# Two token tiles of the first MLP block turned by VectorE instead of TensorE, and a reordering of the attention phase, in a two-layer linear-attention and MLP kernel

## The chip, the cores and the metric

The kernel runs on one core of a Trainium2 chip. The metric is device time of one execution in microseconds (us). Engines are named as in the profile: PE is TensorE, PEld its weight loads, DVE is VectorE, ACT is ScalarE, POOL is GpSimd, and SP is the engine that issues all of this kernel's DMAs, one after the other, from one queue. Each engine takes its instructions strictly in the order in which the program lists them.

## The reference, cut to what matters

The input x has 2048 tokens of 448 features, in float32. Two layers follow each other, each an attention step and an MLP step:

```python
x = x + attention(layernorm(x))       # phi(q) @ (phi(k)^T v), 16 heads of 28, divided by phi(q) . sum(phi(k)), then @ wo
x = x + mlp(layernorm(x))             # gelu(h @ w1 + b1) @ w2 + b2, hidden size 1792
phi = lambda t: where(t > 0, t + 1, exp(t)) + 1e-6
```

Both layers use the same weights. The output has the shape of x.

## The kernel before

**Precision.** A float32 product is made of three fast matmuls. Every operand is split into a high part (a rounded copy, written by ACT) and a low part (the rest, written by DVE or POOL); PE multiplies high by high, high by low and low by high. For the last 64 features two matmuls do.

**Tiles and phases.** The tokens are 16 tiles of 128, and 4 blocks of 4 tiles. A layer has three parts: `phase1` over the 16 tiles, a transition written out as the list of tokens `ORDER` (L491), and the MLP over 4 blocks (L933), in which the attention output of the next block is made beside the MLP of this one (`behind`, L861).

**phase1 (L542).** Step t runs the tokens of a string, `STEP` (L499), with own strings for step 0 and step 1. The tokens, each an operation on one tile:

- `a` takes the layer-norm statistics (DVE bn_stats, bn_aggr, an add; POOL a power, `brs`), `n` normalises (DVE, L383; ACT copies a tail of 64 features for tiles that PE transposes).
- `T` transposes a normalised tile on PE into a PSUM bank (L246); `X` splits it into `XH` (ACT) and `XL` (DVE). The first six tiles of layer 0 go this way. All other tiles are turned by DVE (`tu`, `tv`: L277, L278, 32x32 blocks), stored to DRAM (L283) and read back with the blocks in their places (`sp`, four DMAs, L289); then `X` is `split_t` (L291): ACT L295, DVE L296.
- `K` is the key projection of tile t (11 matmuls), `kp`, `kh`, `kl` its phi and its split (`kl` is DVE L440, followed by the running sum `za`, L444), `s` splits the tile the other way round (ACT L415, POOL L416 and L417), and `G` accumulates x^T phi(k) of tile t-1 in four PSUM banks with tag "acc" (11 matmuls, L479 to L483).
- `Q` is the query projection (11 matmuls) and `qp` its phi, stored to DRAM. Only the first `DEFER` tiles have their query here: 10, so that the six others stand as `Q` in `ORDER`.
- `bg` (layer 0 only) takes `BG[t]` pieces of the MLP weights: a DMA on SP in one step, ACT and POOL splitting it in the next.

Tile 2's transpose takes one of the four "acc" banks (L571), the one that the fourth accumulator of `G` needs next.

**Launch.** In layer 0 the first two tiles go through a hand-written order (`LAUNCH`, L508), and a few lines ahead of it (L896).

**ORDER.** `z`, `gt`, `kv`, `mask`, `m`, `ms` form the matrix M = (masked kv) wo and split it into `Mh` and `Ml`; `qz`, `qs`, `tq`, `qq` scale, transpose and split the queries of block 0; `o` multiplies them by M; `la` adds the residual and takes statistics, `lb` normalises (`o_n`, L744), `T` transposes (L754), `x` splits (L758). Between them stand the deferred `Q`, each followed later by `Qp` (phi on ACT and POOL, L462) or `Qv` (phi on ACT and DVE, L456). `pre` loads the queries of block 1. Then ACT loads the table for gelu (L929) and the MLP starts; its first matmuls need all four split tiles of block 0.

**Buffers that matter.** PSUM: tag "h" has 2 banks (queries, some transposes, MLP hidden), "m" 2, "acc" 4. SBUF: tag "S" has 5 buffers of 128x1024, for weight staging, M, and the turned tiles on their way to DRAM (`sq`) and back (`sp`).

Of the kernel before, what the change touches and what calls it, by code (L numbers as in the profile page):

```python
# [12 lines left out]
OP = mybir.AluOpType  # L13
# [9 lines left out]
def linear_attn_mlp_kernel(  # L23
# [38 lines left out]
    def bank(tag, bufs, name):  # L62
        return psum.tile([128, 512], F32, name=name, tag=tag, bufs=bufs)
# [127 lines left out]
    def ln_bn(xs):  # L191
        st = work.tile([128, 6], F32, name="bst", tag="bst", bufs=2)
        dve.bn_stats(st, xs)
        return st
# [39 lines left out]
    def block(key):  # L234
        if key not in blocks:
            blocks[key] = Block()
        return blocks[key]
# [10 lines left out]
    def split_x(key, j):  # L248
        tp = tps.pop((key, j))
        hi, lo = blocks[key].pieces(j)  # L250
        act.copy(hi, tp)
        dve.tensor_sub(lo, tp, f(hi))
# [35 lines left out]
        for m in range(4):  # L288
            sp.dma_start(r[m * 32:(m + 1) * 32].rearrange("r (i f) -> r i f", i=4), d[m])  # L289

    def split_t(key, t, hi, lo):  # L291

        x = spreads[key, t // 2].rearrange("p (i c u n) -> p u c i n", i=4, c=4, n=32)[:, t % 2]
        h = hi.rearrange("p (c i n) -> p c i n", c=4, n=32)
        act.copy(h, x)  # L295
        dve.tensor_sub(lo.rearrange("p (c i n) -> p c i n", c=4, n=32), x, f(h))  # L296


    def proj(name, key, j, o=None, cs=range(4)):
# [80 lines left out]
    def stage_n(l, t):  # L380

        xs, mv, rs = sts.pop((l, t))
        dve.tensor_scalar(xs, xs, mv[:, 0:1], rs, op0=OP.subtract, op1=OP.mult)  # L383
        xns[l, t] = xs
        if t < TURNED[l]:
            d = tails[l, t] = work.tile([128, 128], F32, name="tail", tag="tail", bufs=2)
            act.copy(d.rearrange("p (u n) -> p u n", u=2), xs[:, None, TL:].to_broadcast([128, 2, 64]))
# [60 lines left out]

    qs_ = {}

    def stage_q(l, t, cs=range(4)):
        qs_[l, t] = proj("q", ("a", l, t // 4), t % 4, qs_.get((l, t)), cs)
        if 3 in cs:
            qo.append((l, t, qs_.pop((l, t))))

    def stage_qphi():  # L456
        while qo:
            l, t, o = qo.pop(0)
            e = phi(o, "eq")
            sp.dma_start(pq_d[l][t * 128:(t + 1) * 128, :], e)  # L460

    def fill_qphi():  # L462

        l, t, o = qo.pop(0)
        e = t512("e", 3, "eq")[:, :D]
        p = t512("E", 2, "ep")[:, :D]
        act.activation(e, o, AF.Relu, scale=-1.0)
        act.activation(p, o, AF.Relu)
# [19 lines left out]

    ORDER = (  # L491
# [4 lines left out]
    )  # L496
    DEFER = NT - ORDER.split().count("Q")

    STEP = "qp K T X s a kp n kh tu kl tv G bg Q ld sp"  # L499
    STEP_0 = "K T X s kp kh kl a n tu Q ld sp"  # L500
    STEP_1 = "T a X qp s kh tu n kl tv G bg ld sp", STEP
    NORM = (
        ((2,), (3, 4), (5, 6), (7,), (8,), (9,), (10,), (11,), (12, 13), (14,), (15,)),
        ((5,), (6,), (7,), (8,), (9,), (10,), (11,), (12, 13), (14,), (15,)),
    )


    LAUNCH = (  # L508
        "kb0 ha0 hb0 ka1 kb1 n1 la0 lb0 K00 T1 K01 ha1 hb1 la1 lb1 ka2 kb2 K10 K11 ka3 kb3 qa0 qb0 K02 K12 K03 K13 "
        "qa1 qb1 qa2 qb2 Q00 Q10 Q01 Q11 Q02 Q12 s0 a2 kp0 qa3 qb3 kh0 n2 kl0 kp1 Q03 Q13"  # L510
    )
    PRE = 5
    BG = [0, 0, 1] + [2] * 5 + [1, 2] + [1] * 6
    LATE = sum(BG)
    loaded = {0: 3}

    def load_to(l, t):
# [24 lines left out]
    def phase1(l, tr):  # L542
        za = consts.tile([128, D], F32, name="za", tag="za")
        acc = []
        load_to(l, NORM[l][1][-1])
        if l == 0:
            launch(za)
            load_to(l, NORM[l][2][-1])
        for t in range(l == 0, NT):
            norm = NORM[l][t] if t < len(NORM[l]) else ()  # L550
            for tok in (STEP_0 if t == 0 else STEP_1[l] if t == 1 else STEP).split():
                if tok == "sp":
                    for u in norm:
                        if u % 2:
                            stage_sp(l, u)
                elif tok == "ld" and t + 2 < len(NORM[l]):
                    load_to(l, NORM[l][t + 2][-1])
                elif tok == "a":
                    for u in norm:
                        stage_a(l, u)  # L560
                elif tok == "n":
                    for u in norm:
                        stage_n(l, u)
                elif tok == "tu":
                    for u in norm[:1]:
                        stage_t(l, u)
                elif tok == "tv":
                    for u in norm[1:]:
                        stage_t(l, u)
                elif tok == "T" and t + 1 < NT:  # L570
                    stage_b(l, t + 1, "acc" if t == 1 else "h")  # L571
                elif tok == "X" and t + 1 < NT and (l == 0 or t + 1 >= 4):
                    stage_x(l, t + 1)
                elif tok == "K":
                    stage_k(l, t)
                elif tok == "qp":
                    stage_qphi()
                elif tok == "kp":
                    stage_kphi(l, t)
                elif tok == "kh":  # L580
                    stage_kh(l, t)
                elif tok == "kl":
                    stage_kl(l, t, za)
                elif tok == "s":
                    stage_s(l, t)
                elif tok == "G" and t >= 1:
                    acc = acc or [bank("acc", 4, f"G{c}")[:, :D] for c in range(4)]
                    stage_g(l, t - 1, acc)
# [56 lines left out]
    def trans_ms(tr, g):  # L645
        if g == 0:
            tr.Mh, tr.Ml = [], []
        if g % 2 == 0:
            for n in ("Mh", "Ml"):
                s = work.tile([128, 1024], F32R, name=n, tag="S", bufs=5)  # L650
                getattr(tr, n).extend(s[:G, i * D:(i + 1) * D] for i in range(2))
        act.copy(tr.Mh[g], tr.mp[g])
        dve.tensor_sub(tr.Ml[g], tr.mp[g], f(tr.Mh[g]))

# [89 lines left out]
    def o_n(l, b, j):  # L744
        t = b * 4 + j
        xn = xns["m", l, t] = ln_norm(sts.pop(("m", l, t)), f"xm{l}_{t}")
        if b == 0:
            act.copy(xn[:, D:], xn[:, TL:D])

    def add_bias(l, b, j):  # L750
# [153 lines left out]
    for l in range(LAYERS):  # L904
# [6 lines left out]
        def pre(j):  # L911
# [3 lines left out]
                background(2)  # L915

        tok_ = SimpleNamespace(
            Q=lambda j: stage_q(l, fill.pop(0)), Qp=lambda j: fill_qphi(), Qv=lambda j: stage_qphi(), G=lambda j: stage_g(l, NT - 1, acc),
            ld=lambda j: (load_pq(l, 0, j), load_x(l, j)), z=lambda j: trans_z(tr, za), gt=lambda j: trans_gt(tr, acc),
            kv=lambda j: trans_kv(tr), mask=lambda j: trans_mask(tr), m=lambda j: trans_m(tr, j),  # L920
            ms=lambda j: trans_ms(tr, j), qz=lambda j: q_z(l, 0, j, tr), qs=lambda j: q_scale(l, 0, j, tr),
            tq=lambda j: q_transpose(l, 0, j), qq=lambda j: q_split(l, 0, j), o=lambda j: o_mm(l, 0, j, tr),
            la=lambda j: o_ln(l, 0, j), lb=lambda j: o_n(l, 0, j), T=lambda j: m_transpose(l, 0, j),
            x=lambda j: m_split(l, 0, j), pre=pre)
# [71 lines left out]
```

## Time and profile before

| what | value |
|---|---|
| time of 3 runs | 881.01, 881.14, 884.27 us; median 881.14 |
| profiled execution | 881.78 us |
| its span (first to last instruction) | 880.1 us |
| granted TensorE clock | 1.000 |
| PE idle by the view of waits | 1.5 + 1.1 + 0.7 + 0.7 + 0.4 us |

The span by stretches (us of the trace, from the views of windows and timeline; busy time in us):

| stretch | what | us | PE | DVE | ACT | POOL | GB/s |
|---|---|---|---|---|---|---|---|
| 0 to 22.59 | launch and step 1, layer 0 | 22.59 | 18.74 | 15.17 | 13.94 | 11.72 | 152 |
| 22.59 to 70.73 | steps 2 to 8 | 48.14 | 48.14 | 38.21 | 31.13 | 25.38 | 189 |
| 70.73 to 104.49 | steps 9 to 15 | 33.76 | 33.72 | 24.50 | 23.70 | 22.27 | 215 |
| 104.49 to 141.18 | ORDER, layer 0 | 36.69 | 36.33 | 26.69 | 17.83 | 13.60 | 104 |
| 444.51 to 536.28 | phase1, layer 1 | 91.77 | 91.67 | 68.06 | 51.67 | 28.34 | 157 |
| 536.28 to 572.94 | ORDER, layer 1 | 36.66 | 36.30 | 26.67 | 16.89 | 11.35 | 80 |

A row of the timeline gives start, duration, engine, line, operation, tiles, shapes, count and, in brackets, the idle time of the engine before it and what the profile holds for its end. Matmuls overlap: one of 448 columns is listed with 0.37 us, but in a row of them each starts 0.20 us after the one before. So the pace of PE is read from the differences of starts, and a stall of less than about 0.17 us does not show as idle time.

### The profile page before, as it was taken

Reading aid. Unit: us, or ns where it says so; the run is one execution under the profiler, and the core shown is the slowest. Engines: PE = TensorE matmul, PEld = TensorE weight load, DVE = VectorE, ACT = ScalarE, POOL = GpSimd, SP = SyncE. Lnnn points to the kernel's source line nnn. Section 1 sums busy time; section 2 is a strip of 40 time slices with the busy share of each in tenths; the row PEclk is TensorE's granted clock in tenths of the full one; section 3 lists DMA queues with packets and bytes.
Section 4 is the critical chain, followed back from the end, with each engine's and each line's share of the span. In section 5 each row is a group of like instructions: output and inputs, shape, how many; then the busy total and the mean of one; then the engine's idle time right before and its main releaser. Section 6 shows DMA issues by size and latency. Waiting matters only on the chain.

```text
span 880.1 us, 11693 instructions
## 1 busy us (share of the span) xinstructions
PE 871.8 (99%) x4190; PEld 773.4 (88%) x4190; DVE 485.6 (55%) x947; ACT 344.8 (39%) x609; POOL 221.1 (25%) x252
## 2 busy tenths in 40 slices
PE   8999999999999999999999999999999999999998
PEld 6999988888888888888899999888888888888887
DVE  6878585658455543226467866755574473432112
ACT  6576645324223322333355664442233133223221
POOL 5466633335012102011222333220220140140000
PEclk9999999999999999999999999999999999999999
DMA  5477715624413402051146443243332323111001
GB/s 156 148 213 223 218 53 159 199 78 140 132 59 104 156 0 96 1 178 48 48 136 196 153 144 95 63 152 101 104 114 91 112 75 131 49 49 40 3 1 42
DMA packets 62762, 93.71 MB, mean 106 GB/s; under 512 B 8816, under 2 KB 57968, under 8 KB 62704
## 3 DMA queue, kind: packets, MB, share of 16 engines
q1 hardware_dynamic: 62704, 92.97, 33.7%
q8 instruction: 33, 0.54, 0.3%
q14 instruction: 25, 0.20, 0.1%
HBM read 55.65 MB, written 34.08 MB: 102 GB/s over the span
## 4 chain that ended last, share of the span: by engine, by line
PE 96%; DVE 1%; POOL 1%; DMA 1%; ACT 1%; issue 0%; SPq 0%; POOLq 0%; ACTq 0%; DVEq 0%
PE y L806 10%; PE y L805 10%; PE y L804 10%; PE hp L787 9%; PE hp L786 9%; PE hp L788 9%; PE hp L789 3%; PE hp L790 3%; PE G L480 2%; PE G L481 2%; PE G L479 2%; PE psk L306 2%; PE psk L308 2%; PE psk L307 2%; PE psq L306 2%; PE psq L307 2%
## 5 line engine op out<-in xcount | busy, mean ns | idle before, releaser
L796 DVE TENSOR_TENSOR gl<-g,gh 128x512 fp32r<-128x512 f32 x112 | 82.7, 738 | 299.7 <-ACT gh L795 299.7
L792 ACT ACTIVATE g<-hp,b1s 128x512 f32<-128x512 f32 x112 | 77.0, 688 | 406.4 <-PE hp L790 406.4
L806 PE MATMUL y<-w2h,gl 128*128 128x448 f32 x448 | 163.9, 366 | 0.0
L805 PE MATMUL y<-w2l,gh 128*128 128x448 f32 x448 | 163.8, 366 | 0.0
L804 PE MATMUL y<-w2h,gh 128*128 128x448 f32 x448 | 163.8, 366 | 0.0
L787 PE MATMUL hp<-XH,w1l 128*128 128x512 f32 x336 | 131.7, 392 | 0.0
L786 PE MATMUL hp<-XH,w1h 128*128 128x512 f32 x336 | 131.4, 391 | 0.0
L788 PE MATMUL hp<-XL,w1h 128*128 128x512 f32 x336 | 131.2, 391 | 0.0
L203 POOL TENSOR_TENSOR brs<-bve,mhalf 128x1 f32<-128x1 f32 x64 | 38.9, 607 | 272.5 <-DVE bve L201 265.4
L804 PEld LDWEIGHTS y<-w2h,gh 128*128 128x128 f32 x448 | 84.2, 188 | 8.8
L805 PEld LDWEIGHTS y<-w2l,gh 128*128 128x128 f32 x448 | 84.3, 188 | 8.3
L806 PEld LDWEIGHTS y<-w2h,gl 128*128 128x128 f32 x448 | 84.3, 188 | 6.5
L788 PEld LDWEIGHTS hp<-XL,w1h 128*128 128x128 f32 x336 | 63.1, 188 | 13.6
L787 PEld LDWEIGHTS hp<-XH,w1l 128*128 128x128 f32 x336 | 63.2, 188 | 11.1
L786 PEld LDWEIGHTS hp<-XH,w1h 128*128 128x128 f32 x336 | 63.3, 188 | 10.9
L795 ACT CAST gh<-g 128x512 fp32r<-128x512 f32 x112 | 69.7, 622 | 3.6
L416 POOL TENSOR_TENSOR xnl<-x,xnh 128x384 fp32r<-128x384 f32 x32 | 35.7, 1117 | 84.4 <-ACT xnh L415 50.0
L683 POOL TENSOR_TENSOR pz<-pq,zb 128x448 f32<-128x448 f32 x32 | 36.6, 1148 | 79.7 <-DVE dn L689 65.3
L296 DVE TENSOR_TENSOR XL<-sp,XH 128x512 fp32r<-128x512 f32 x50 | 42.7, 861 | 5.3 <-ACT XH L295 5.3
L790 PE MATMUL hp<-XL,w1x 128*128 128x512 f32 x112 | 43.6, 389 | 0.0
L789 PE MATMUL hp<-XH,w1x 128*128 128x512 f32 x112 | 43.6, 389 | 0.0
L752 POOL TENSOR_TENSOR x<-x,b2b 128x448 f32<-128x448 f32 x32 | 41.9, 1332 | 0.0
(145 smaller groups left out, 1565.6 us busy)
## 6 DMA issues: line engine op xcount, KB each, us to landing
x<-in_A_x_dram SPq DMA_DIRECT2D x32, 224.0 KB, 3.7
pq_d<-eq SPq DMA_DIRECT2D x32, 224.0 KB, 2.9
pq<-pq_d SPq DMA_DIRECT2D x32, 224.0 KB, 3.2
x<-x_d SPq DMA_DIRECT2D x32, 224.0 KB, 3.6
sq_a<-sq SPq DMA_DIRECT2D x13, 512.0 KB, 2.9
sp<-sq_a SPq DMA_DIRECT2D x52, 128.0 KB, 3.0
sq_q<-sq SPq DMA_DIRECT2D x12, 512.0 KB, 2.6
sp<-sq_q SPq DMA_DIRECT2D x48, 128.0 KB, 3.1
```

Of the source, the lines that this page charges most:

```text
L296: dve.tensor_sub(lo.rearrange("p (c i n) -> p c i n", c=4, n=32), x, f(h))
L786: pe.matmul(o, w1h[:, c, s], x.moving(x.hi, c), start=(c == 0), stop=False)
L787: pe.matmul(o, w1l[:, c, s], x.moving(x.hi, c), start=False, stop=False)
L788: pe.matmul(o, w1h[:, c, s], x.moving(x.lo, c), start=False, stop=False)
L789: pe.matmul(o, w1x[:, s], x.moving(x.hi, 3), start=False, stop=False)
L790: pe.matmul(o, w1x[:, s], x.moving(x.lo, 3), start=False, stop=True)
L792: act.activation(g, hp, AF.Gelu_apprx_tanh, bias=b1s[:, i:i + 1])
L795: act.copy(gh, g)
L796: dve.tensor_sub(gl, g, f(gh))
L804: pe.matmul(acc[j], gh[:, s], w2h[:, i], start=first, stop=False)
L805: pe.matmul(acc[j], gh[:, s], w2l[:, i], start=False, stop=False)
L806: pe.matmul(acc[j], gl[:, s], w2h[:, i], start=False, stop=last)
```

## The change

- **Launch.** Ahead of it, tile 0 is normalised (and its tail copied by ACT) before ACT splits the first key weight. In `LAUNCH`, `la0` (the low part of tile 0's first half) stands ahead of `n1`.
- **Step 1 of layer 0.** `X` of tile 2 stands ahead of the statistics; only tile 3 is taken in this step, tile 4 moves to step 2; the phi of the two first queries (`q1`) is spread out, the second one ahead of the normalisation of tile 3. Step 2 of layer 0 has its own string, with three tiles' statistics and the key's phi between them.
- **All other steps** from 2 in layer 0 and from 1 in layer 1: `kl` stands ahead of `tu`.
- **Queries.** Seven are deferred, so step 9 has no `Q`. In `ORDER` one `Q` stands between `o2` and `o3`, one after `o3`, and the last two (`Qa`) write to "acc" banks. The third `Qp` stands ahead of `ms0`; four queries now have their phi by `Qv`.
- **Block 0's tiles 0 and 1** in both layers: `tu0`, `tu1`, one store, one read back (`st`, `sp`), and `split_t` in place of PE's transposes `T0`, `T1` and of `split_x`; for tile 0 the subtraction is made by POOL. ACT copies no tail for them. `pre` moves behind `x2`.
- **Buffers.** The last two rows of `Ml` go to "F" buffers, and `sq`, `sp` of block 0 take two "S" buffers.
- **BG** in layer 0: step 8's entry stays 1, step 9 takes 1 piece instead of 2, and step 12 takes 2 instead of 1.

```diff
-    def split_t(key, t, hi, lo):
+    def split_t(key, t, hi, lo, eng=dve):
...
-        dve.tensor_sub(lo.rearrange("p (c i n) -> p c i n", c=4, n=32), x, f(h))
+        eng.tensor_tensor(lo.rearrange("p (c i n) -> p c i n", c=4, n=32), x, f(h), op=OP.subtract)
...
-    def stage_q(l, t, cs=range(4)):
+    def stage_q(l, t, cs=range(4), tag=None):
+        if tag:
+            qs_[l, t] = bank(tag, 4, "psq")[:, :D]
...
-        "m0 qq1 Qp m1 qz3 ms0 qq0 m2 ms1 m3 ms2 tq2 ms3 qs3 o0 la0 qq2 o1 tq3 lb0 la1 qq3 Qp pre "
-        "o2 T0 lb1 la2 o3 x0 T1 Q lb2 la3 x1 T2 Q x2 lb3 Qp "
-        "T3 x3 Qp Q Qv "
+        "m0 qq1 Qp m1 qz3 Qp ms0 qq0 m2 ms1 m3 ms2 tq2 ms3 qs3 o0 la0 qq2 o1 tq3 lb0 tu0 la1 qq3 "
+        "o2 lb1 tu1 st la2 Q o3 sp Qv1 lb2 la3 Q T2 lb3 Qv1 x2 pre Qa x0 x1 T3 x3 Qa Qv "
     )
-    DEFER = NT - ORDER.split().count("Q")
+    DEFER = NT - sum(tok in ("Q", "Qa") for tok in ORDER.split())
-    STEP = "qp K T X s a kp n kh tu kl tv G bg Q ld sp"
-    STEP_0 = "K T X s kp kh kl a n tu Q ld sp"
-    STEP_1 = "T a X qp s kh tu n kl tv G bg ld sp", STEP
+    STEP = "qp K T X s a kp n kh kl tu tv G bg Q ld sp"
+    STEPS = {
+        (0, 1): "T X a3 q1 s kh q1 n3 kl G bg ld sp",
+        (0, 2): "K T X s a4 kp n4 a5 kh kl n5 a6 n6 tv G bg Q ld sp",
+        (1, 0): "K T X s kp kh kl a n tu Q ld sp",
+    }
...
-        "kb0 ha0 hb0 ka1 kb1 n1 la0 lb0 K00 T1 K01 ha1 hb1 la1 lb1 ka2 kb2 K10 K11 ka3 kb3 qa0 qb0 K02 K12 K03 K13 "
+        "kb0 ha0 hb0 ka1 kb1 la0 n1 lb0 K00 T1 K01 ha1 hb1 la1 lb1 ka2 kb2 K10 K11 ka3 kb3 qa0 qb0 K02 K12 K03 K13 "
...
-    BG = [0, 0, 1] + [2] * 5 + [1, 2] + [1] * 6
+    BG = [0, 0, 1] + [2] * 5 + [1] * 4 + [2] + [1] * 3
...
-            for n in ("Mh", "Ml"):
+            for n in ("Mh", "Ml")[:1 if g else 2]:
...
+        if g >= 2:
+            tr.Ml.append(t512("F", 2, "Ml", F32R)[:G, :D])
...
-        if b == 0:
+        if b == 0 and j >= 2:
             act.copy(xn[:, D:], xn[:, TL:D])
...
-        split_x(("m", l, b), j)
+        if j < 2:
+            split_t(("m", l, b), j, *block(("m", l, b)).pieces(j), dve if j else pool)
+        else:
+            split_x(("m", l, b), j)
...
     bn = ln_bn(xt[0, 1])
+    stage_n(0, 0)
     split_hi("k", 0, st_k)
-    stage_n(0, 0)
...
+            x=lambda j: m_split(l, 0, j), tu=lambda j: turn(xns.pop(("m", l, j)), ("m", l, 0), j),
+            st=lambda j: store_sq(("m", l, 0), 0), sp=lambda j: spread(("m", l, 0), 0), pre=pre)
```

More of the change, by code (lines that the diff above doesn't have):

```diff
@@ L454, in stage_q, with stage_qphi @@
             qo.append((l, t, qs_.pop((l, t))))
-    def stage_qphi():
-        while qo:
+    def stage_qphi(n=9):
+        for _ in qo[:n]:
             l, t, o = qo.pop(0)
@@ L492, in linear_attn_mlp_kernel @@
         "Q ld1 z ld0 ld2 qz0 qz1 G gt qs1 Q Qp kv qs0 tq1 Q mask qz2 tq0 qs2 ld3 "
[3 rows of a table removed]
-    )
-    DEFER = NT - ORDER.split().count("Q")
-    STEP = "qp K T X s a kp n kh tu kl tv G bg Q ld sp"
-    STEP_0 = "K T X s kp kh kl a n tu Q ld sp"
-    STEP_1 = "T a X qp s kh tu n kl tv G bg ld sp", STEP
[2 rows of a table added]
+    )
+    DEFER = NT - sum(tok in ("Q", "Qa") for tok in ORDER.split())
+    STEP = "qp K T X s a kp n kh kl tu tv G bg Q ld sp"
+    STEPS = {
[3 rows of a table added]
+    }
     NORM = (
-        ((2,), (3, 4), (5, 6), (7,), (8,), (9,), (10,), (11,), (12, 13), (14,), (15,)),
+        ((2,), (3,), (5, 6), (7,), (8,), (9,), (10,), (11,), (12, 13), (14,), (15,)),
         ((5,), (6,), (7,), (8,), (9,), (10,), (11,), (12, 13), (14,), (15,)),
@@ L544, in phase1 @@
         acc = []
-        load_to(l, NORM[l][1][-1])
+        load_to(l, 4 if l == 0 else NORM[l][1][-1])
         if l == 0:
@@ L550, in phase1 @@
             norm = NORM[l][t] if t < len(NORM[l]) else ()
-            for tok in (STEP_0 if t == 0 else STEP_1[l] if t == 1 else STEP).split():
-                if tok == "sp":
+            for tok in STEPS.get((l, t), STEP).split():
+                if tok[1:].isdigit() and tok[0] in "an":
+                    (stage_a if tok[0] == "a" else stage_n)(l, int(tok[1:]))
+                elif tok == "q1":
+                    stage_qphi(1)
+                elif tok == "sp":
                     for u in norm:
@@ L917, in linear_attn_mlp_kernel @@
         tok_ = SimpleNamespace(
-            Q=lambda j: stage_q(l, fill.pop(0)), Qp=lambda j: fill_qphi(), Qv=lambda j: stage_qphi(), G=lambda j: stage_g(l, NT - 1, acc),
+            Q=lambda j: stage_q(l, fill.pop(0)), Qp=lambda j: fill_qphi(), Qv=lambda j: stage_qphi(j or 9),
+            Qa=lambda j: stage_q(l, fill.pop(0), tag="acc"), G=lambda j: stage_g(l, NT - 1, acc),
             ld=lambda j: (load_pq(l, 0, j), load_x(l, j)), z=lambda j: trans_z(tr, za), gt=lambda j: trans_gt(tr, acc),
@@ L923, in linear_attn_mlp_kernel @@
             la=lambda j: o_ln(l, 0, j), lb=lambda j: o_n(l, 0, j), T=lambda j: m_transpose(l, 0, j),
-            x=lambda j: m_split(l, 0, j), pre=pre)
+            x=lambda j: m_split(l, 0, j), tu=lambda j: turn(xns.pop(("m", l, j)), ("m", l, 0), j),
+            st=lambda j: store_sq(("m", l, 0), 0), sp=lambda j: spread(("m", l, 0), 0), pre=pre)
         for tok in ORDER.split():
```

## The prediction, made before the changed kernel was run

> **What bounds the kernel now.** The page first: is one engine always busy?
>
> ```profile
> span 880.1 us, 11693 instructions
> PE 871.8 (99%) x4190; PEld 773.4 (88%) x4190; DVE 485.6 (55%) x947; ACT 344.8 (39%) x609; POOL 221.1 (25%) x252
> ```
>
> PE is, so a gain is PE work taken away or a PE stall closed. The view of waits of PE lists the stalls:
>
> ```profile
> PE G L482 <- POOL brs L203: 1.5, 1, 1.5
> ...
> PE psq L306 <- ACT ep L468: 0.7, 2, 0.4
> PE tp L246 <- ACT tail L387: 0.7, 1, 0.7
> ```
>
> Overlapped durations hide part of each stall, so I go to the timeline and take differences of starts: 0.20 between 448-column matmuls, 0.44 for a tile's four transposes. The largest stall (timelines of PE and DVE):
>
> ```profile
> 20.27 0.37 PE L481 MATMUL G<-kh,xnl 128*128 128x448 f32 x1
> 22.11 0.44 PE L482 MATMUL G<-kh,xnh 128*128 128x448 f32 x1 [1.47 <-POOL brs L203]
> ...
> 20.35 0.62 DVE L193 BATCH_NORM_STATS2 bst<-x 128x6 f32<-128x448 f32 x1
> ...
> 21.28 0.68 DVE L252 TENSOR_TENSOR XL<-tp,XH 128x512 fp32r<-128x512 f32 x1
> ```
>
> The profile blames `brs`, which nothing here reads. L482 opens the fourth accumulator, in the bank where tile 2's transpose lies until `XL` is done: 21.28 + 0.68 = 21.96. `XL` stood behind the statistics of two tiles. The starts are 1.84 apart instead of 0.20, and L483 follows 0.08 late: 1.7 us lost.
>
> In ORDER (both layers alike; layer 1's row stands at 570.46):
>
> ```profile
> 137.73 0.60 PE L246 MATMUL tp<-ident,xm 128*128 128x128 f32 x4
> 138.69 0.47 PE L306 MATMUL psq<-wq,XH 128*128 128x448 f32 x1 [0.36 <-ACT ep L468]
> 139.00 0.36 PE L307 MATMUL psq<-wq,XH 128*128 128x448 f32 x1
> ```
>
> The last query waits for its "h" bank, whose reader stands behind tile 3's normalisation on ACT. 0.96 instead of 0.44, and 0.31 instead of 0.20: 0.63 us a layer.
>
> **The change, part by part** (us; starts "as before" are the trace's)
>
> *Transposes.* T0 and T1 go from PE: 2 tiles x 2 layers x 0.44 = **-1.76**. In their place stand DVE work and a trip through DRAM. What must be late next is the MLP's first matmul, which needs all eight pieces. PE's new order from o1's end (126.75): tq3 0.44, o2 2.47, Q 2.23, o3 2.47, Q 2.23, T2 0.44, Qa 2.23, T3 0.44, Qa 2.23: MLP at 141.9 (141.18 + 2.23 for the query that came from step 9 - 0.88 - 0.63 agrees). Its first use of a low piece is two matmuls later, 142.4.
> The chain of tile 1, with rows of ORDER: o1 126.75; DVE is held until 127.85 by tile 0's turn (L277 and L278, 0.50 + 0.20 by starts); `la1` 1.65 to 129.5; ql3, brs (0.55) and xm to 130.7; turn to 131.4. Store: the page's median for `sq_a` is 2.9, so 134.3. Four reads issued over 1.3 (SP's rows at 76.29), each landing 3.0 after its issue: 138.6. ACT then makes XH0, XH1, XH3 (0.5 each by starts) until 140.5. POOL's XL0: 128x448 takes 1.15 (L470), so 512 columns some 1.3, an estimate; DVE's XL1 (0.69) and XL3 (0.69). All done by 141.4: **1.0 us of slack**, cost nothing. What SP has between: two query stores of 0.43 issue each behind the reads, and `pre`'s six loads behind those; nothing waits for them until POOL's `pz` (0.8 later than before) and the turn at 150.60 that follows. The "S" buffer of that turn is now the first half of Mh, read by DMAs that land by 150.2: no wait over 1, and DVE has 4 us there before PE needs the next `gl`.
> Bounds: POOL never subtracts a strided 512 tile in this trace. Nearest rows: 1.0 (128x384, L416) and 3.05 for two of 128x448 (L134), 1.5 each, 1.75 scaled to 512. I take 1.3. A turned tile's L296 is 0.68 in the median and 1.64 at most:
>
> ```profile
> L296 DVE TENSOR_TENSOR XL<-sp,XH x50: 669/684/1643, 45.9 to 799.5; 128x512 fp32r<-128x512 f32 x50
> ```
>
> The slow ones, such as 84.91 with 1.53, run beside POOL's w1l and xnl. Here XL1 runs beside XL0: done with it at 141.4 at the latest, then XL3 142.0. Still ahead of 142.4.
> The Trainium skill (SBUF — State Buffer, "Who interferes with whom") has a rule behind that row: a VectorE operation with two SBUF inputs and a GpSimd operation that reads SBUF exclude each other for a whole instruction. By that rule XL1 simply starts when XL0 ends, and XL3, with one input in PSUM, is free of it; the sum stays. By those rows 0 to 0.6 per layer is the bound for this edit, and I take 0.
>
> *The last query's bank.* Qa writes to "acc", where o0 and o1 have long been read: the stall of 0.63 goes in both layers: **-1.26**. The third Qp moves ahead of ms0: ACT gets 3 x 0.43 = 1.3 there. Mh3 then ends near 122.0 on before's clock and Ml3 near 122.8; o0's last group needs them at 123.6 to 123.9. Covered, by about 1.
>
> *Launch.* The tail of tile 0 is copied at 5.7 instead of 6.59, so the fourth transpose starts near 6.1 instead of 6.93. The first half of XL, wk and x1 are then a chain: kb0 stays at 6.71 to 7.33 (ACT's wk before it starts at 6.12, when its DMA has landed), la0 7.63, n1 8.1, tile 1's transposes at 8.1 instead of 8.77 with the tail 0.6 earlier. POOL's run of splits (10.59 to 16.90 without a gap) starts earlier by as much, and brs, n2 and T2 follow it: **-0.6**; bounds 0 (a weight DMA is late) and -0.83.
>
> *Step 1.* XL of tile 2 goes ahead of the statistics and is done at 19.5, where L482 wants it at 19.9: **-1.7**. But the next reader comes early too. K(2) ends at 22.5, and T3 needs x3, which now stands on DVE behind the second query's phi, and that behind ACT: from XH at 18.2, ACT has two phis, xnh and kh, 3.7 in before's rows, to 21.9; L320 to 22.6; L383 to 23.0. PE waits 0.5: **+0.55**. Bounds 0 and 1.
>
> *kl ahead of tu.* On DVE the turn is 0.7. The stalls that it closes:
>
> ```profile
> 83.18 0.58 DVE L277 STREAM_TRANSPOSE sq<-x 128x384 f32<-128x384 f32 x1
> ...
> 83.87 0.58 DVE L440 SCALAR_TENSOR_TENSOR kl<-psk,kh 128x448 fp32r<-128x448 f32 x1
> ...
> 84.51 0.48 PE L480 MATMUL G<-kl,xnh 128*128 128x448 f32 x1
> ```
>
> and the same at 458.34. By starts 0.3 and 0.36. Layer 1: kl has its input at 456.94, could end at 457.6, wanted at 458.1: **-0.36**. The price is a store issued 1.0 later (kl and za, 0.5 each), in a layer where XL is 4.4 ahead: nothing.
>
> *Step 9 without a query, layer 0.* The query's 2.23 moves into ORDER (counted above, neutral), but steps 9 to 15 now come 2.23 earlier for everything that doesn't. There the trace has little to give:
>
> ```profile
> 74.40 0.62 ACT L295 CAST XH<-sp 128x512 fp32r<-128x512 f32 x1 [2.17 <-DMA sp<-sq_a]
> ...
> 75.05 0.69 DVE L296 TENSOR_TENSOR XL<-sp,XH 128x512 fp32r<-128x512 f32 x1 [1.74 <-ACT XH L295]
> ...
> 77.42 0.36 PE L306 MATMUL psk<-wk,XH 128*128 128x448 f32 x1
> ```
>
> XL of tile 10 ends at 75.75, 2.07 before the matmul at 77.8 that reads it: 2.23 are wanted. Its reads were issued at 67.92 and landed 5 later; its store now issues 1.0 later (the turn behind kl), the reads perhaps 0.4. Stall 0.2 to 0.6. Then kl of step 9 ended 0.58 ahead of its matmul: 2.23 less 0.7 (no turn ahead of it) leaves 0.7 more after that shift; step 10 is spared the phi of query 9 (1.1 of ACT), 0.15 more. Steps 12 to 14 run at PE's 4.46 with two weight pieces in one: about 0.2. Sum 1.2, less the 0.3 stall that before had here: **+0.9**. Bounds: -0.3 (the reads land with the PE's shift and nothing waits) and +2.2. Layer 1 has 4.4 at this place and loses nothing.
>
> **Sum.** -1.76 - 1.26 - 0.6 - 1.7 + 0.55 - 0.36 + 0.9 = -4.2. The profiled execution took 881.78 (span 880.1 and 1.7 around it): 877.6. It lies 0.64 above the median of 881.14; from the median it is 876.9. I give **877.3**.
>
> **Rivals.**
> *Layer 0 keeps pace* (0.33). The wait at 74.40 is one slow landing: 5 us where other reads take 3. If it shifts with the rest, the +0.9 becomes -0.3: 877.3 - 1.2 = **876.1**. For it: SP's order around it is that of before. Against it: reads wait for a store that is 1.0 later.
> *The turned tiles just miss the MLP* (0.12). XL0 at twice my price, or reads landing 1 late: with 1.0 of slack some 1.0 a layer is lost: **879.3**.
> *The trip through DRAM falls into a full queue* (0.05): slower than before. The store issued at 50.07 let its read-back go at 55.68, 5.6 later instead of 2.9; the read-back issued at 67.92 let ACT go at 74.40, 6.5 instead of 4.3. Both at once in ORDER: 2.7 + 2.2 - 1.0 of slack = 3.9 a layer, 7.8 in all: **885.1**. It decides against the change from 2.1 per layer on, that is, when store and reads together take 3.1 longer than 7.3. Against it: ORDER's traffic is 104 and 80 GB/s, where those stretches had 189, and `pre` now comes later, so that SP is nearly empty from 121 to 131.
> *The change does not do what it says* (0.05): some wait that L482's example shows to be misnamed is another's, and half of the stalls (1.7, 1.26) stay: 877.3 + 1.5 = **878.8**.
>
> **How the numbers follow.** My forecast has 0.45, the rivals 0.33, 0.12, 0.05 and 0.05. Range for 8 in 10: from 875.6 (pace kept, launch at its end of 0.83) to 880.0 (the +2.2 bound, or the missed MLP); the full queue is left out. Measurement tells about 0.5% from no change here, that is 4.4 us: under 876.7 is faster. All of the pace rival and a part of the forecast's own scatter fall there: faster 0.40, within 0.56, slower (over 885.5, only the queue at its worst) 0.04.
>
> **What would show it.** PE's transposes of `xm` 16 instead of 32; no idle at L482, T3 near 23.0 waiting for DVE; no wait for `ep`; XL of tile 10 and `kl` of steps 9 and 10 as the waits of layer 0; L788 of each layer's first block without a wait on POOL or DVE. I am wrong if the first MLP matmuls of a layer wait, or if steps 2 to 8 lose PE's pace to step 2's three tiles.

## The result, and the profile after

The changed kernel took 881.1 us (median of 22 runs, 879.77 to 882.68), the kernel before 882.43 beside it (22 runs, 880.78 to 884.27): a ratio of 0.9986, 95% interval 0.9980 to 0.9993. The profiled execution took 880.54, 1.24 less than before's 881.78. Forecast were -4.2 us and 875.6 to 880.0; about a third came.

The page and the view of waits of PE, after:

```profile
span 878.8 us, 11689 instructions
PE 872.6 (99%) x4174; PEld 770.4 (88%) x4174; DVE 489.9 (56%) x957; ACT 342.7 (39%) x601; POOL 220.6 (25%) x250
...
PE psk L306 <- ACT XH L295: 0.4, 1, 0.4
PE G L482 <- DVE kl L440: 0.4, 2, 0.2
PE tp L246 <- DVE x L383: 0.3, 1, 0.3
```

The long waits of before (1.5 at the fourth accumulator, 0.7 for `ep`, 0.7 for `tail`) are gone, and 16 instructions of PE with them. Yet PE is busy for 0.8 us longer than before: it waits in pieces too short for the idle column, which only the differences of starts show.

So I cut both traces at the same instructions. K(t) is the first key matmul of step t, z the first matmul of ORDER's token `z` (one query stands ahead of it in ORDER), "MLP" the first matmul of the MLP with the waits of its next five added. Ahead of z stand 11 queries before and 10 after; one is 11 matmuls of 0.20, 2.23.

| stretch | before | after | difference | forecast |
|---|---|---|---|---|
| start to K(2), layer 0 | 22.59 | 20.30 | -2.29 | -2.3 |
| K(2) to K(3) | 7.13 | 7.81 | +0.68 | +0.55 |
| K(3) to K(9) | 41.01 | 41.40 | +0.39 | 0 |
| K(9) to z, less a query's 2.23 in before | 33.77 | 36.74 | +2.97 | +0.9 |
| z to MLP, plus that query in before | 36.52 | 35.15 | -1.37 | -1.51 |
| K(0) of layer 1 to its MLP | 128.29 | 126.62 | -1.67 | -1.87 |

Layer 1 gave most of what was forecast. Layer 0 was 2.3 ahead at K(2) and 0.4 behind at its MLP. Most of that went in steps 9 to 15. The lines that answer to those of XL of tile 10 and of `kl` (timelines of ACT, DVE and PE, after):

```profile
73.88 0.62 ACT L295 CAST XH<-sp 128x512 fp32r<-128x512 f32 x1 [2.07 <-DMA sp<-sq_a]
...
74.53 0.69 DVE L296 TENSOR_TENSOR XL<-sp,XH 128x512 fp32r<-128x512 f32 x1 [1.63 <-ACT XH L295]
...
74.55 0.47 PE L306 MATMUL psk<-wk,XH 128*128 128x448 f32 x1 [0.41 <-ACT XH L295]
...
77.41 0.62 DVE L440 SCALAR_TENSOR_TENSOR kl<-psk,kh 128x448 fp32r<-128x448 f32 x1
...
78.08 0.47 PE L482 MATMUL G<-kl,xnh 128*128 128x448 f32 x1 [0.18 <-DVE kl L440]
```

PE wants tile 10 at 73.97 (77.42 before), but `XH` starts only 0.52 earlier than before. By starts K(10) comes 0.58 late, and its third matmul 0.22 more, since that reads `XL`; `kh` and `kl` cost G(9) 0.8 in all. Then follow 0.1 in each of steps 11 and 12, 0.3 in step 13 and 0.9 in step 15, for the most part at `kl` and `XL`.

### The profile page after: what moved, and what is told of

Its sections match the earlier page's. It is cut to its first block, busy times and chain, and to the rows that moved or that the text cites. A ratio compares the mean times of both kernels' runs of the same rounds, so it can differ in the third digit from the quotient of the medians.

```text
span 878.8 us, 11689 instructions
## 1 busy us (share of the span) xinstructions
PE 872.6 (99%) x4174; PEld 770.4 (88%) x4174; DVE 489.9 (56%) x957; ACT 342.7 (39%) x601; POOL 220.6 (25%) x250
## 4 chain that ended last, share of the span: by engine, by line
PE 89%; DMA 4%; DVE 3%; ACT 1%; SPq 1%; issue 1%; POOL 1%; ACTq 0%; POOLq 0%; DVEq 0%
PE y L821 10%; PE y L820 10%; PE y L819 10%; PE hp L802 9%; PE hp L801 9%; PE hp L803 9%; PE hp L804 3%; PE hp L805 3%; PE psq L308 2%; PE psq L306 2%; PE psq L307 2%; PE op L744 2%; PE op L743 2%; PE op L745 2%; DMA sq_a<-sq 1%; DMA sp<-sq_a 1%
## 5 line engine op out<-in xcount | busy, mean ns | idle before, releaser
L296 DVE TENSOR_TENSOR XL<-sp,XH 128x512 fp32r<-128x512 f32 x52 | 45.4, 879 | 10.7 <-ACT XH L295 10.7
```

Of the source, the lines that this page charges most:

```text
L296: eng.tensor_tensor(lo.rearrange("p (c i n) -> p c i n", c=4, n=32), x, f(h), op=OP.subtract)
```

## The experiments

In the table, "extra" is K(9) to z beyond the value that four undisturbed runs share to 0.01 (b1, e7, e9 and e10: 35.67 with 11 queries ahead; with 10 it is counted from 33.44, a query less). The kernel before has 0.33, the changed kernel 3.30. "L0 end" is layer 0's MLP as above. A ratio is to runs of the kernel before on the same chip.

| run | ratio, 95% interval | K(2) | extra | z to MLP | L0 end |
|---|---|---|---|---|---|
| e1 query back in step 9 | 1.0005, 0.9995 to 1.0015 | 20.68 | 1.84 | 36.12 | 143.56 |
| e2 turn first | 0.9990, 0.9979 to 1.0000 | 20.58 | 2.62 | 36.25 | 142.13 |
| e3 two tiles a step | 1.0001, 0.9991 to 1.0011 | 20.45 | 2.23 | 35.21 | 140.76 |
| b1 before, split first | 0.9997, 0.9985 to 1.0008 | 20.54 | 0.00 | 34.26 | 139.93 |
| e6 = e2 + e3 | 0.9981, 0.9972 to 0.9990 | 20.84 | 0.96 | 36.13 | 140.94 |
| e7 = e6, query back | 0.9980, 0.9970 to 0.9989 | 20.21 | 0.00 | 36.10 | 141.41 |
| e8 = e6, kl first from step 9 | 0.9982, 0.9972 to 0.9992 | 20.73 | 2.77 | 36.32 | 142.68 |
| e9 layer 1 alone | 0.9975, 0.9965 to 0.9984 | 22.36 | 0.00 | 34.26 | 140.43 |
| e10 base = e9, split first | 0.9971, 0.9960 to 0.9982 | 21.20 | 0.00 | 34.31 | 140.63 |
| e11 base, kl first in layer 0 | 0.9986, 0.9976 to 0.9995 | 20.49 | 1.77 | 34.31 | 141.68 |
| e12 base, three tiles | 0.9970, 0.9959 to 0.9981 | 20.57 | 0.70 | 34.31 | 140.57 |
| e13 base, no query in step 9 | 0.9986, 0.9978 to 0.9995 | 20.65 | 3.56 | 36.55 | 143.63 |
| e15 = e13, piece moved | 0.9994, 0.9984 to 1.0004 | 20.78 | 1.45 | 36.83 | 141.91 |
| e14 changed, read-back first | 1.0180, 1.0164 to 1.0196 | 20.27 | 14.84 | 36.22 | 160.25 |
| e16 = e13, read-back first | 1.0155, 1.0138 to 1.0172 | 20.79 | 11.70 | 36.43 | 155.35 |
| e17 = e6, read-back first | 1.0141, 1.0123 to 1.0160 | 20.15 | 13.23 | 35.14 | 154.77 |
| e18 changed kernel again | 0.9994, 0.9985 to 1.0002 | 20.52 | 2.27 | 36.15 | 142.17 |
| e19 base, launch, three tiles | 0.9970, 0.9958 to 0.9982 | 20.16 | 1.09 | 34.31 | 140.45 |

My theory after the traces: turned tiles run in a loop (DVE turn, store, read-back, ACT's `XH`, the statistics and the next turn). Two edits make it later against PE, `kl` ahead of the turn and three tiles in step 2, and the step without a query lets that show. Rivals: a lead from launch is given back whatever is done; the missing query is enough by itself.

### Undoing parts in the changed kernel

**e1**, in layer 0 alone:

```diff
-    DEFER = NT - sum(tok in ("Q", "Qa") for tok in ORDER.split())
+    ORDERS = (ORDER.replace(" la2 Q ", " la2 "), ORDER)
+    DEFERS = [NT - sum(tok in ("Q", "Qa") for tok in o.split()) for o in ORDERS]
```

> The changed kernel, but in layer 0 six queries are deferred as before: step 9 has its query again, and none stands between o2 and o3 there (layer 1 stays as changed). The changed kernel measured 0.9986 of before (-1.3 us). Theory A (the loop of the turned tiles, from DVE's turn over DRAM to ACT's split, keeps its own pace in layer 0's phase1, and a query taken out of step 9 is a PE cover lost): the stalls at the key matmuls of tile 10 and at G in steps 10 to 15, 3.0 us together, fall under 1.0; the MLP of layer 0 then waits 1.2 to 2.0 for the turned tiles, since ORDER lost its cover; in all 0.5 to 1.5 faster than the changed kernel, ratio to before 0.9970 to 0.9980. Theory B (the weights' splits at 4.46 us a step cost it, query or not): the stalls of steps 11 to 15 stay, 1.3 us, and the ratio is 0.9985 to 1.0005.

The extra fell to 1.84 only, and without the query between O 2 and O 3 the MLP itself waits: no gain (theory A had asked for 0.9970 to 0.9980).

**e2**, `STEP` of layer 0 with `tu` ahead of `kl` again:

```diff
+    STEP_0 = "qp K T X s a kp n kh tu kl tv G bg Q ld sp"
```

> The changed kernel with tu ahead of kl again in layer 0 (layer 1 keeps kl ahead). If the order kl, tu is what makes the read-backs late (every store 1.0 us later, theory C): ACT's split of tile 10, at 73.88 in the changed kernel, starts at 72.5 to 73.2, the wait of the key matmul of tile 10 falls from 0.8 to under 0.3; but kl is 0.7 later in steps 9 and 10, so G waits more there; in all -0.5 to +0.3 against the changed kernel, ratio to before 0.998 to 0.999. If the order does not matter to the loop, tile 10's split stays within 0.3 of 73.88 and the kernel is 0.3 to 0.8 slower than the changed one (ratio 0.999 to 0.9995), from kl alone.

**e3**, steps 1 and 2 as before but for `X` ahead:

```diff
-        (0, 1): "T X a3 q1 s kh q1 n3 kl G bg ld sp",
-        (0, 2): "K T X s a4 kp n4 a5 kh kl n5 a6 n6 tv G bg Q ld sp",
+        (0, 1): "T X a qp s kh tu n kl tv G bg ld sp",
-        ((2,), (3,), (5, 6), (7,), (8,), (9,), (10,), (11,), (12, 13), (14,), (15,)),
+        ((2,), (3, 4), (5, 6), (7,), (8,), (9,), (10,), (11,), (12, 13), (14,), (15,)),
```

> The changed kernel, but steps 1 and 2 of layer 0 take tiles 3 and 4, then 5 and 6, in the order of before, with the split of tile 2 still ahead of the statistics. Theory A: what PE has as a lead by step 2 is given back by step 10, so a change of the lead does not matter: PE waits about 1.3 longer for tile 3's transposes, the turn of tile 7 is about 1 us earlier, and the waits of steps 9 to 14 shrink by as much; start of ORDER and total within 0.4 of the changed kernel, ratio to before 0.998 to 0.999. Rival (the lead is kept by what follows): 1.0 to 1.4 slower than the changed kernel, ratio 1.000.

The extras, 2.62 and 2.23, are not told from that of a second execution of the changed kernel itself (e18, 2.27), and neither edit lowers the time: 0.9990 and 1.0001, the latter the ratio that e3's rival had named. e3's profiled execution, 880.14, was the fastest of its twelve (median 882.1), so that its trace shows it too well.

**b1**, the kernel before with one token moved:

```diff
-    STEP_1 = "T a X qp s kh tu n kl tv G bg ld sp", STEP
+    STEP_1 = "T X a qp s kh tu n kl tv G bg ld sp", STEP
```

> The kernel before with one edit: in step 1 of layer 0 the split of tile 2 stands ahead of the statistics. By starts 1.7 us of stall at L482 go. Theory A (the lead is given back in layer 0, the loop sets the end of phase1): ORDER of layer 0 starts within 0.5 of before, total 0 to -0.5, ratio 0.9994 to 1.0. Rival (a stall closed early in phase1 is a gain at the end, as I predicted for the change): after 0.8 lost at tile 3's transposes, total -0.8 to -1.2, ratio 0.9987 to 0.9991.

In this one execution layer 0 ends 1.1 earlier than before's, which speaks against "given back whatever is done". The time of twelve runs, 0.9997, speaks for it. The profiled execution lost 1.6 in layer 1 in another way (see the last section); whether that holds for the twelve isn't shown. Of the 1.8 that K(2) is earlier than in e9, whose layer 0 is before's, 1.3 goes at once, at tile 3's transposes (K(2) to K(3) is 8.45 for 7.13).

**e6, e7, e8** put e2 and e3 together, then bring the query back (as e1 does), or put `kl` first from step 9 on.

> The changed kernel with two edits in layer 0 undone: DVE turns the tile ahead of kl again in every step, and steps 1 and 2 take tiles (3, 4) and (5, 6) again; the split of tile 2 stays first, step 9 has no query, the two first tiles are turned by DVE. Theory D (the loop of turn, store, read-back and ACT's split was made 2 to 3 us later against TensorE by kl ahead of the turn and by three tiles in one step; step 9 without a query then shows it as stalls): stores near 36.2, 49.3 and 63.1, no wait of K(10) for XH or XL; G(9) and G(10) wait for kl, 1 to 2 us together; first MLP matmul of layer 0 at 139.0 to 140.0 (141.25 in the changed kernel); time 0.9965 to 0.9985 of the kernel before. Rival R (the two edits are no cause; one query less ahead of z by itself opens the gaps): steps 10 to 15 lose 2.5 us or more again, first MLP matmul at 140.5 or later, ratio 0.9980 to 1.0005.

> As the run with turn first and two tiles a step, and besides layer 0 has its query in step 9 again (none between O 2 and O 3). Layer 0 up to z is then the kernel before with the split of tile 2 first. Theory D: no stall over 0.5 in steps 10 to 15, z at 105.4 to 105.9 with 11 queries ahead of it; first MLP matmul at 138.2 to 139.4 and a stall of 0.7 to 1.3 behind it for the low half of the turned tiles; ratio 0.9955 to 0.9980. Rival R (layer 0's reordering gives nothing whatever the steps are): first MLP matmul with its stall at 140.5 or later, ratio 0.9985 or more.

> As the run with turn first and two tiles a step, but in layer 0 kl goes ahead of the turn from step 9 on, where the query is left out and the last tiles are turned. Theory D: stores 36.2, 49.3 and 63.1 as there, G(9) and G(10) wait less for kl (under 0.8 together), the store of tile 15 is up to 1.0 later; first MLP matmul of layer 0 at 138.3 to 139.6; ratio 0.9955 to 0.9975, the fastest of the four. Rival R: stalls of steps 10 to 15 at 2.5 us or more, ratio 0.9980 to 1.0005.

e6 brings the extra to 0.96 and e7 to 0, as the loop theory wants, but the end of layer 0 does not come as early as I expected: z to MLP takes 36.1 in both. With the same queries b1 takes 34.26 where e7 takes 36.10. In e7 the transition waits for DVE and ACT (timeline of PE):

```profile
129.82 0.47 PE L735 MATMUL op<-Mh,ql 112*128 112x448 f32 x1 [0.83 <-DVE ql L723]
140.19 0.50 PE L802 MATMUL hp<-XH,w1h 128*128 128x512 f32 x1 [0.37 <-ACT XH L251]
141.77 0.47 PE L804 MATMUL hp<-XL,w1h 128*128 128x512 f32 x1 [0.85 <-DVE XL L252]
```

By starts 1.0, 0.5 and 1.0. Turning two tiles on DVE pays in the transition only with a query between O 2 and O 3, and that query has to come out of steps 9 to 15. e8's extra of 2.77 missed its expectation, with the time of e6 (0.9982 and 0.9981).

### Adding parts to a quiet base

**e9** has layer 0 of before (`ORDER_0` is before's `ORDER`; its launch, step strings, tiles and `BG` too) and layer 1 of the change.

```diff
+    ORDERS = ORDER_0, ORDER
...
-        if j < 2:
+        if l and j < 2:
```

> The changed kernel with layer 0 as in the kernel before: launch, order of steps, tiles per step, query in step 9, first two tiles of block 0 through TensorE. Only layer 1 has the change. Theory D (layer 1 gives all that was forecast for it, and what the changed kernel keeps is no more than layer 1's): layer 0 as before within 0.3 us, layer 1 from its first K to the first MLP matmul 1.8 shorter, the end 1.6 to 2.0 earlier, ratio 0.9975 to 0.9987, equal to the changed kernel's or below it. Rival (layer 1 gives about 0.5, and the other half comes from layer 0): ratio 0.9990 to 0.9998.

As forecast (layer 0 alone ended 0.6 earlier than before's, where 0.3 was the bound), and no slower than the whole change, though its wait of 1.5 at the fourth accumulator is still there:

```profile
PE G L484 <- POOL brs L203: 1.5, 1, 1.5
```

**e10** is e9 with b1's token. **e11** adds `STEP_0 = STEP`. **e12** adds the step strings and tiles that e3 takes out. **e13** moves step 9's query:

```diff
-        "o2 T0 lb1 la2 o3 x0 T1 Q lb2 la3 x1 T2 Q x2 lb3 Qp "
+        "o2 T0 lb1 la2 Q o3 Qp x0 T1 Q lb2 la3 x1 T2 Q x2 lb3 Qp "
```

> Layer 1 with the change, layer 0 as in the kernel before but for one token: the split of tile 2 goes ahead of the statistics in step 1. Base of this set: from K(2) to z 85.1 (as the kernel before with that one token), first MLP matmul of layer 0 0.4 to 0.6 ahead of the run with layer 1 alone (139.8 to 140.1), the end at 877.2 to 877.9. Theory D: ratio 0.9965 to 0.9980, the fastest so far. Rival (what the split first gains is taken back ahead of the first MLP matmul): no earlier than the run with layer 1 alone there, ratio as that one's or above.

> The base (layer 1 with the change, split of tile 2 first) with one addition: kl ahead of the turn in layer 0's steps 2 to 15. Step 9 keeps its query. Theory D: stores 0.6 to 1.0 later each than in the base, K(2) to z longer by 0.3 to 1.2, ratio 0.0003 to 0.0013 above the base. Rival (kl first is free as long as step 9 keeps its query): K(2) to z within 0.2 of the base, equal time.

> The base with one addition: step 1 takes tile 3 alone and step 2 tiles 4, 5 and 6, as in the changed kernel (step 2 alone has kl ahead of the turn). Theory D: the first stores 0.8 to 1.5 later than in the base, K(2) to z longer by 0.3 to 1.3, less 0.3 that the shorter wait of T3 gives; ratio 0.0002 to 0.0013 above the base. Rival (it pays for itself by T3's shorter wait): K(2) to z equal or shorter, equal time or below.

> The base with one move: in layer 0 the query of step 9 goes to between O 2 and O 3, the first two tiles of block 0 still through TensorE. This is the forecast's term for step 9 without a query by itself: K(2) to z comes out at 85.1 less 2.23 plus the term, z to the first MLP matmul 2.2 longer. Theory D (0.9 was about right as long as the turned tiles come as early as here): term 0.8 to 1.4, ratio 0.0008 to 0.0016 above the base. Rival (leaving the query out costs 2.5 to 3.3 by itself, whatever the order of the steps): K(2) to z at 85.4 or more, ratio 0.0025 or more above the base.

e10 is not told from e9 (0.9971 and 0.9975), and its layer 0 ends no earlier (140.63 and 140.43): its rival, by which the early split is taken back, fits. Its K(2) came 0.66 later than b1's with the same code: launch scatters by that much. e11 is slower than the base by 0.0015, with the query still in step 9. Its loop shows why. ACT and SP in e10, then in e11:

```profile
50.62 0.38 SPq L283 DMA_DIRECT2D sq_a<-sq  x1
64.10 0.33 SPq L283 DMA_DIRECT2D sq_a<-sq  x1
...
73.47 0.62 ACT L295 CAST XH<-sp 128x512 fp32r<-128x512 f32 x1 [1.46 <-DMA sp<-sq_a]
```

```profile
52.49 0.33 SPq L283 DMA_DIRECT2D sq_a<-sq  x1
66.01 0.33 SPq L283 DMA_DIRECT2D sq_a<-sq  x1
...
74.87 0.62 ACT L295 CAST XH<-sp 128x512 fp32r<-128x512 f32 x1 [2.15 <-DMA sp<-sq_a]
```

K(2) of e11 is 0.71 earlier, and its stores are 1.9 later: 2.6 against PE, where `kl` and `za` are 1.0 of DVE a step. I put the rest down to the loop: a later read-back holds ACT, and what ACT does behind it holds the next turn. That is argued; a loop that does not move with PE would also turn the 0.71 of K(2) into lateness. e12's extra of 0.70 is paid by a shorter wait of T3 (7.75 from K(2) to K(3) for 8.45): equal time, the rival. e13 has an extra of 3.56 where I expected 0.8 to 1.4, and a time 0.0015 above the base, which is in the range that I expected (0.0008 to 0.0016).

**e15** gives e13 the changed kernel's `BG`.

> The run with the base and no query in step 9 (K(9) to z 37.0, an excess of 3.6), with the changed kernel's numbers of weight pieces: step 9 has one piece instead of two, step 12 two instead of one. Tells whether the 2.6 between that run and the one with turn first and two tiles (excess 1.0) is the piece. Theory P (ACT's and SP's second piece in step 9 fills the place that the query's phi left): excess 0.5 to 1.7, ratio 0.0010 to 0.0030 below that run's 0.9986. Theory L (the read-back of tiles 10 and 11, which lands ahead of step 9's pieces, came 1.1 later in that execution): the excess goes with the read-back's landing, 1 to 3.6, and the ratio stays within 0.0010 of 0.9986.

The extra is 2.1 less and the time no better (0.9994). The two are alike up to step 9, and yet `XH` of tile 10 came 0.8 apart, e13 ahead of e15 here (timelines of ACT):

```profile
74.10 0.62 ACT L295 CAST XH<-sp 128x512 fp32r<-128x512 f32 x1 [2.57 <-DMA sp<-sq_a]
```

```profile
73.31 0.62 ACT L295 CAST XH<-sp 128x512 fp32r<-128x512 f32 x1 [1.70 <-DMA sp<-sq_a]
```

So the extra of one execution is good to a microsecond or two, and only many executions give its mean: e13 and e15 lie 0.0015 and 0.0023 above the base, 1.3 and 2.0 us, with intervals of about 0.001 on each ratio.

### Moving the read-back in SP's order

**e14**, one token in layer 0 of the changed kernel; **e16** and **e17** the same in e13 and e6:

```diff
+    STEP_0 = "qp K T X s a kp n kh kl tu tv G sp bg Q ld"
```

> The changed kernel with one token moved in layer 0: SP issues the read-back of the turned tiles ahead of the step's weight pieces and of x's load, not behind them. No instruction is added or left out. In the undisturbed runs K(9) to z takes 33.4 with 10 queries ahead (35.67 less one query of 2.23); the changed kernel has 36.7, an excess of 3.3. Theory L (the loop through DRAM sets it: ACT waits in order for read-backs that land behind weight pieces): the last read-back of tiles 10 and 11 lands 1.5 to 3 earlier after its store than the 8.7 of the changed kernel, K(10) doesn't wait for XH, the excess falls to 1.0 to 2.3, ratio 0.9960 to 0.9980. Rival Q (one query less leaves DVE and ACT too slow for TensorE, wherever the read-backs land): the excess stays at 2.7 or more, ratio 0.9980 or more.

> The run with the base and no query in step 9, with the read-back ahead of the weight pieces in SP's order. Theory L: no wait of K(10) for XH, excess from 3.6 down to 0.5 to 2.0, ratio 0.9965 to 0.9980. Rival Q: excess 2.7 or more, ratio 0.9980 or more.

> The run with turn first and two tiles a step (excess 1.0, ratio 0.9981), with the read-back ahead of the weight pieces in SP's order. Theory L: excess 0.2 to 1.0; G(9)'s wait for kl stays, 0.3 to 0.8; DVE is the bound of the transition behind z, so that z to the first MLP matmul stays at 36.0 to 36.3 and the gain at the end is under 0.7; ratio 0.9970 to 0.9981. Rival Q: excess 1.0 or more, ratio 0.9981 or more.

All three are slower, by 14 to 17 us against the kernels that they were made from. Neither theory foresaw it, and the loop theory as I wrote it falls: it had the read-backs as the late part and the weight pieces as their traffic. The pieces are in the loop themselves. SP waits for the store to land before it issues the read-back, so the pieces behind it go out later, and ACT takes its work in order (e14, timelines of ACT and PE, then the windows of 69 to 72 and 85 to 89: PE, weight loads, DVE, ACT, POOL, clock, DMA share, GB/s):

```profile
82.14 1.15 ACT L341 CAST w1h<-stg 128x448 fp32r<-128x448 f32 x2 [5.63 <-DMA stg<-in_B_w_dram]
...
84.90 0.74 PE L306 MATMUL psk<-wk,XH 128*128 128x448 f32 x1 [4.53 <-ACT XH L295]
```

```profile
69.00:72.00 3.00, 3.00 (x10) 2.55 (x9) 2.64 (x7) 2.70 (x6) 1.84 (x3) 0.50 0.76 242
85.00:89.00 4.00, 4.00 (x11) 3.44 (x12) 3.72 (x9) 1.96 (x4) 1.86 (x4) 0.50 0.59 160
```

The tile's read-back had landed at 79.5; `XH` stood behind `w1h`, whose piece landed at 82.1. From store to store the loop took 16.8 and 17.2 (14.0 and 13.3 in the changed kernel). That the order of the loop's DMAs moves the time is shown. The corrected theory has ACT's order as its core; no run tested it.

### The changed kernel again, and the best version

> The changed kernel, unaltered, for a second profile and as the yardstick of the next run on the same chip. The losses of steps 9 to 15 in layer 0 (3.3 in the first profile) are read from single executions, and the executions of one kernel lie up to 3 apart. Theory L (the loss belongs to the kernel; its size moves with the read-backs' landings): 1.5 to 4.5 again, with waits for XH of tile 10 and for kl; ratio 0.9978 to 0.9995. Rival S (the first profile was an unlucky execution): under 1.0, and the first MLP matmul of layer 0 under 139.5.

> The base with three tiles in step 2 and the changed kernel's launch: layer 1 and all edits of launch and steps 1 and 2 in layer 0, but query in step 9, turn ahead of kl and order of the transition as in the kernel before. Theory L: excess under 1.0, first MLP matmul of layer 0 at 139.8 to 140.6, ratio 0.9960 to 0.9980, below the changed kernel on the same chip. Rival (the layer-0 edits that are left out were worth something): ratio 0.9984 or more, or no less than the changed kernel's.

e18 has an extra of 2.27, with the same waits for `XH` of tile 10 and `kl`: the loss is the kernel's. Its z to MLP is 1.0 longer than in the first profile. There DVE turns tile 1 at 131.10, 25.1 behind z (130.29 and 24.0 in the first profile), its `XL` of tile 3 ends at 142.38, and the MLP's first low piece starts only at 142.52. e19 keeps the launch, the early split and the three tiles in layer 0, and the whole of layer 1. It took 879.28 (878.71 to 880.45) beside 881.31 (880.25 to 882.53) of the changed kernel on the same chip: the lowest median of all, 0.9970 of before. It is not told from e9, e10 and e12 (0.9975 to 0.9970). The layer 0 of these four ends at 140.43 to 140.63, whether K(2) stands at 22.36 or at 20.16: what launch, early split and three tiles gain at K(2) is gone by the MLP, and no gain of theirs is shown in the time. What e19 has over before is layer 1's, as far as the runs tell.

## Why the prediction was wrong, point by point

- **Step 9 without a query, layer 0 (+0.9): failed.** It measured +3.0 and, in e18, +1.9 (2.27 less before's 0.33). The working priced tile 10 and one `kl`, with everything ahead of step 9 moving along with PE, and the later store as "the reads perhaps 0.4". In the trace the turned tiles' path did not move along. PE's K(9) came 1.2 earlier, and the stores of tiles 8 and 9 and of tiles 10 and 11 later (timelines of SP, before and after):

```profile
50.07 0.38 SPq L283 DMA_DIRECT2D sq_a<-sq  x1
...
64.52 0.33 SPq L283 DMA_DIRECT2D sq_a<-sq  x1
```

```profile
51.84 0.33 SPq L283 DMA_DIRECT2D sq_a<-sq  x1
...
65.10 0.33 SPq L283 DMA_DIRECT2D sq_a<-sq  x1
```

  Against PE that is 3.0 and 1.8. The 3.0 did not go through: the first of these stores took 5.5 to land in before, so that its read-back was issued at 55.68; in the changed kernel it was issued at 54.87. The later pair carries tile 10, whose `XH` came 0.5 earlier where PE wanted it 3.45 earlier (73.97 for 77.42). On the base, `kl` first costs 0.0015 of the time and the missing query 0.0015 to 0.0023, each by itself. With the three tiles the changed kernel has an extra of 2.3 to 3.3 us, and undoing `kl` first and three tiles (e6) leaves 1.0 in one profile. How the rest divides between these two is open: e2 and e3 alone gained no time.
- **kl ahead of tu: half right.** In layer 1 the 0.36 came and the price was nothing (phase 1 is 91.41 for 93.99, 2.58 less, of which 2.23 is the query). In layer 0, "a store issued 1.0 later" was counted at 0.4 once; in e11 the stores are 1.0, 2.6 and 2.6 later against PE, 0.7 of which is K(2).
- **Launch and step 1 (-2.3): right at K(2), by chance in its parts, and not kept.** K(2) is at 22.59 and 22.36 with neither edit, at 20.49 to 21.20 with the split first alone, at 20.15 to 20.84 with both. The split is worth 1.8 on the means (forecast 1.7), launch 0.3 (0.6). The sum took this lead, less T3's 0.55, for a gain at the end. With the transition of before it was gone by layer 0's MLP in e10, e12 and e19 and in b1 0.5 of it was left (layer 0's ends against e9's). In the changed kernel a part of the loss in steps 9 to 15 can be this lead given back; the runs do not separate it.
- **T3's wait (+0.55): right, and not all.** By starts it was 0.51. Step 2's three tiles also hold DVE when the third query wants a bank: 0.35 more at 32.85, which the text had named as a way to be wrong and priced at nothing.
- **Transposes and bank (-1.51 a layer): right in layer 1, by luck in layer 0.** In layer 1 z to MLP is 1.3 less in the first profile, and 1.0 to 1.3 less in every later one that has the new layer 1. In layer 0 it is 1.37 less in the first profile but 0.37 in e18; of the eight profiles with this transition three have 35.1 to 35.2 and five 36.1 to 36.3, where before has 36.52. The slack of 1.0 was not there: `XL` of tile 3 ends at 141.64, and the matmul that reads it, due at 141.72, starts at 141.78 (POOL, DVE and PE, after):

```profile
139.19 1.29 POOL L296 TENSOR_TENSOR XL<-sp,XH 128x512 fp32r<-128x512 f32 x1 [2.96 <-PE tp L246]
...
139.66 1.37 DVE L296 TENSOR_TENSOR XL<-sp,XH 128x512 fp32r<-128x512 f32 x1 [0.29 <-ACT XH L295]
...
140.96 0.68 DVE L252 TENSOR_TENSOR XL<-tp,XH 128x512 fp32r<-128x512 f32 x1
...
141.78 0.47 PE L803 MATMUL hp<-XL,w1h 128*128 128x512 f32 x1
```

  POOL's 1.29 was forecast at 1.3. DVE's subtraction took 1.37 where 0.68 is the median. The rule of the Trainium skill (SBUF — State Buffer, "Who interferes with whom"), by which such a pair excludes each other, agrees: DVE's row ends at 141.03, 0.55 after POOL's. The working had this collision in its bound, with 0.4 of slack left, and took the MLP of before to start at 141.18; it starts at 141.02.
- **The rivals.** "Keeps pace" was given 0.33 and is the one that the runs contradict most: the wait at 74.40 was no single slow landing but came back in all the profiles read for it, with 0.8 to 2.6. "Just miss the MLP" (some 1.0 a layer) happened in layer 0: its first matmuls wait 0.15 in the first profile and 0.7 to 0.8 in e18, e2 and e6, with z to MLP 1.0 longer; layer 1 lost at most 0.3 of its gain by it. "Full queue" did not. None named the loop, and the range ended 1.1 below the median. What makes DVE a microsecond later in layer 0's transition in five profiles of eight is open.

## What to carry to other kernels

A part that leaves the bottleneck engine is worth no more than the work beside that engine allows: before pricing such an edit, follow one item through its whole loop (here turn, store, read-back, in-order ACT, next turn) and ask whether the loop moves with the engine or stays. An operation put ahead of another in a loop can cost more than its duration: 1.0 became 2.6 in e11. A stall closed early is a gain only if nothing behind it takes the lead back, so follow it to the end of the phase. Where executions differ by as much as the effect, take the mechanism from the trace and the size from many timed runs, and test the halves of a change apart: one layer's half was no worse than the whole.

## What the runs showed of the hardware

**Two paces of the same matmuls.** In layer 1's steps, with no wait and a granted clock of 1.00, 448-column matmuls start every 0.2027 us in the profile of before and every 0.2067 in that of b1. PE, before and then b1, eight matmuls apart:

```profile
470.00 0.37 PE L306 MATMUL psk<-wk,XH 128*128 128x448 f32 x1
...
471.62 0.37 PE L479 MATMUL G<-kh,xnh 128*128 128x448 f32 x1
```

```profile
469.75 0.37 PE L306 MATMUL psk<-wk,XH 128*128 128x448 f32 x1
...
471.41 0.37 PE L479 MATMUL G<-kh,xnh 128*128 128x448 f32 x1
```

Over some 400 matmuls that is 1.6 us. Of 25 runs of the kernel before on one chip, 10 lie between 881.05 and 881.70, 15 between 882.57 and 883.90, none between. That these are the two paces is argued, not shown. With the new layer 1 all profiles had the short one there. e18 had the long one from 40 to 70 us, which by estimate is 0.6 of what it lost there. The cause is open.

**Half clock after short waits.** In e14 PE waited 2.2 us at 64.9, and from 69 to 72 its granted clock was 0.50; in e17 waits of 1.8 and 0.6 were followed by 0.50 from 104 to 107. The Trainium skill (TensorE: Matmul & The Clock Gate, "HAM oscillation — how this bites in real kernels") has idle gaps above some 3.4 us as the cause. Here shorter ones came before it, and it began about 2 us after PE had started again. Each time matmuls started every 0.37 us instead of 0.20 for 3.4 us, some 1.5 us more by estimate.
